# Seven-product layer 2 with gates folded into the input, in a fused attention and mixture-of-experts kernel

## Chip, cores and metric

The kernel runs on one core of one Trainium2 chip (TRN2). The metric is the device time of one execution in microseconds (us). The times quoted are medians of several executions. A profile is one execution, and its span is about 2 us shorter than that execution's time. TensorE is the matmul engine (PE in the profile; PEld is its weight load), VectorE is DVE, ScalarE is ACT, GpSimd is POOL, and SP issues most DMA transfers.

## The reference

Attention comes first: 8 batches, 8 heads, 512 local and 32 global tokens, head size 64. Local tokens see a window of 32 on each side and all global tokens. The 8 x 544 = 4352 tokens of 512 features then go through 8 experts, weighted by a gate that eight Sinkhorn iterations make.

```python
def _moe_ref(x, w_gate, w1, w2):              # x: [4352, 512], w1: [8, 512, 1024], w2: [8, 1024, 512]
    P = np.exp(x @ w_gate - max)              # [4352, 8]
    for _ in range(8):                        # Sinkhorn
        P /= P.sum(1, keepdims=True) + 1e-09
        P /= P.sum(0, keepdims=True) + 1e-09
        P *= N / E
    for e in range(E):
        h = np.maximum(x @ w1[e], 0.0)        # layer 1
        out += P[:, e:e + 1] * (h @ w2[e])    # layer 2, gated
```

All gates are positive, so P * relu(x w1) w2 is the same as relu((P * x) w1) w2. The change uses this.

## The kernel before

Three stages follow each other. (a) and (b): attention, 32 steps, one for each pair of heads; the two layers of expert 0, which need no gate yet, are cut into units that a `filler` puts between the attention instructions as soon as their tokens exist. After the last step come the Sinkhorn iterations, with more filler. (c): experts 1 to 7 over groups of 512 tokens.

```python
# (a), (b): one attention step s (pair s; the "back" of pair s-2; the "attend" of pair s-1)
if s < NP: scores(s, 0)
fill_in()
if s > READY and (s - READY - 1) % HP == 0: gate(...)       # writes the PSUM bank `gbank`, read by an exponential
if s + 1 < NP: transposes(s + 1)                            # q and k of the next pair, evicted by VectorE
if 0 <= p < NP: back(p)                                     # writes `gbank` too
if s < NP and s % 2 == 1: global_keys(b, hp // 2)           # scores of local queries against global keys
fill_in()
if s < NP: scores(s, 1); masks(s)
...
if s == HP + 2: global_prep(1)        # 12 of the 16 global blocks prepared in one piece, at pair 6
# loads: q in pieces of 256 bytes, k in pieces of 1 KB, v in pieces of 256 bytes; all global tensors at the start
```

```python
# (c): layer 1 and layer 2 of experts 1 to 7, 512 tokens at a time
def layer1(k):
    ...
    for dk in range(DP):
        nc.tensor.matmul(ph[:, ff, 0:TG], w1e[:, dk, P * fm : P * (fm + 1)], xT[:, dk, P * g0 : P * g0 + TG], ...)
    # ReLU out of PSUM: half on ScalarE, half on VectorE
def layer2(k, hT):
    for c in range(gn):               # 128 tokens: 8 matmuls of 512 columns
        for fk in range(FT):
            nc.tensor.matmul(py, hT[:, fk, P * c : P * (c + 1)], ws[e][1][:, fk, :], ...)
        nc.vector.scalar_tensor_tensor(out=out_of(to), in0=py, scalar=P_nat[:, to, e : e + 1],
                                       in1=out_of(to), op0=ALU.mult, op1=ALU.add)   # gate and add, in SBUF
```

The softmax here doesn't subtract the row's maximum and nothing guards it: scores larger than these inputs give would overflow.

Of the kernel before, what the change touches and what calls it, by code (L numbers as in the profile page):

```python
# [13 lines left out]
PSUM = bass.MemoryType.PSUM  # L14


@with_exitstack
def kernel(
# [42 lines left out]
    fill = ctx.enter_context(tc.tile_pool(name="fill", bufs=2))  # L61
    ps_mm = ctx.enter_context(tc.tile_pool(name="ps_mm", bufs=2, space=PSUM))
# [6 lines left out]
    TA = 20  # L69
    outA = persist.tile([P, TA, D], FP32)  # L70
    w1_0 = persist.tile([P, DP, F], FP16)
    w2_0 = persist.tile([P, FT, D], FP16)
    outB_box = []

    def out_of(to):
        return outA[:, to, :] if to < TA else outB_box[0][:, to - TA, :]
# [34 lines left out]
    def y_unit(g, c):  # L111
        g0, gn = groups[g]
        py = ps_mm.tile([P, D], FP32, tag="mm", name="py")
        for fk in range(FT):
            nc.tensor.matmul(py, hTs[g][:, fk, P * c : P * (c + 1)], w2_0[:, fk, :],  # L115
                             start=(fk == 0), stop=(fk == FT - 1))
        copy_to(out_of(g0 + c), py)
# [25 lines left out]
    with tc.tile_pool(name="const", bufs=1) as const, \  # L143
# [15 lines left out]
        g16 = [const.tile([P, 2 * B, Dh], FP16, name=f"g16{i}") for i in range(2)]  # L159

        stage, nat = {}, {}
        scr = outA.rearrange("p t d -> p (t d)")
        QW = H * 4 * Dh
        for n, nm in enumerate(("q", "k", "v")):
            stage[0, nm] = scr[:, QW * n : QW * (n + 1)].rearrange("p (j d) -> p j d", d=Dh)
        GW = 2 * B * Dh
        gst = [scr[:, 3 * QW + GW * n : 3 * QW + GW * (n + 1)].rearrange("p (j d) -> p j d", d=Dh) for n in range(3)]
        srcs = {"q": q_l, "k": k_l, "v": v_l}

        def load(b, nm, h0=0, h1=H):  # L170
            if (b, nm) not in stage:
                stage[b, nm] = ld.tile([P, H * NM, Dh], FP32, tag=nm + "s", name=nm + "s")
            src = srcs[nm][b, h0:h1]
            o = stage[b, nm][:, NM * h0 : NM * h1, :]
            if nm == "q":
                nc.sync.dma_start(out=o, in_=src.rearrange("h (t p) d -> p (h t) d", p=P))
            elif nm == "k":
                nc.sync.dma_start(out=o.rearrange("p (h so) d -> p h (so d)", so=4),  # L178
                                  in_=src.rearrange("h (p so) d -> p h (so d)", so=4))
            else:  # L180
                for so in range(4):
                    nc.sync.dma_start(out=o[32 * so : 32 * (so + 1)],  # L182
                                      in_=src.rearrange("h (m n so) d -> so n (h m) d", n=32, so=4)[so])
# [14 lines left out]
        def transposes(p):  # L198
            b, hp = divmod(p, HP)
            pt = ps_t.tile([P, 2, Sl], FP16, tag="t", name="pt")  # L200
            for t in range(NM):
                nc.tensor.transpose(pt[:, 0, P * t : P * (t + 1)], nat[b, "q"][:, t, 2 * hp : 2 * hp + 2, :], identity)  # L202
# [4 lines left out]
            nc.vector.tensor_copy(out=t, in_=pt)  # L207
# [120 lines left out]
        def load_g(j0, j1, eng):  # L328
            for n, src in enumerate((q_g, k_g, v_g)):
                eng.dma_start(out=gst[n][:, j0:j1, :],  # L330
                              in_=src.rearrange("b (hh hq) s d -> (hq s) (b hh) d", hq=4)[:, j0:j1, :])

        load_g(0, JA, nc.scalar)
# [8 lines left out]
        load_g(JA, 2 * B, nc.sync)  # L342
        make_identity(nc, identity)
        nc.vector.memset(gqbd, 0.0)
# [13 lines left out]
        nc.gpsimd.tensor_copy(out=vga[:, 0:JA, 0:Dh], in_=gst[2][:, 0:JA, :])  # L358
        nc.gpsimd.dma_start(out=w_gate_sb, in_=moe_w_gate.rearrange("(dko dki) e -> dki dko e", dki=P))
        tick = const.tile([P, 2], FP32)  # L360
        nc.gpsimd.tensor_copy(out=tick[:, 0:1], in_=stage[0, "v"][:, H * NM - 1, 0:1])
        nc.gpsimd.dma_start(out=w1_0, in_=moe_w1[0].rearrange("(dko dki) f -> dki dko f", dki=P))
        nc.gpsimd.tensor_copy(out=tick[:, 1:2], in_=stage[1, "k"][:, 0, 0:1])
        nc.gpsimd.dma_start(out=w2_0, in_=moe_w2[0].rearrange("(fko fki) d -> fki fko d", fki=P))

        def global_prep(part):
            j0, j1 = ((0, JA), (JA, 2 * B))[part]
            n = j1 - j0
            ceng = (nc.scalar.copy, nc.vector.tensor_copy)
            for i in (0, 1):  # L370
                ceng[i](out=g16[i][:, j0:j1, :], in_=gst[i][:, j0:j1, :])
            if part:
                nc.gpsimd.tensor_copy(out=vga[:, j0:j1, 0:Dh], in_=gst[2][:, j0:j1, :])
            JC = 4
            for j in range(j0, j1, JC):
                pq = ps_mm.tile([P, 2, 2 * JC, Sg], FP32, tag="mm", name="pq")
                for a in (0, 1):
                    for jj in range(JC):
                        flip(pq[:, a, 2 * jj : 2 * jj + 2, :], g16[a][:, j + jj, :])
                for i in (0, 1):  # L380
                    ceng[i](out=gqbd[Dh * i : Dh * (i + 1), 2 * j : 2 * (j + JC), Sg * i : Sg * (i + 1)],
                            in_=pq[Dh * i : Dh * (i + 1), 0])
                nc.scalar.copy(out=kgT[:, 2 * j : 2 * (j + JC), :], in_=pq[:, 1])
            pgg = ps_mm.tile([P, n, Sg], FP32, tag="mm", name="pgg")
# [10 lines left out]
        global_prep(0)  # L395

        LAG = 1
        READY = HP + LAG + 1
        FA = 2.6
        gA = TA // GT - 1  # L400
        for s in range(NP + LAG + 2):
            b, hp = divmod(s, HP)
            have = min((s - READY) // HP, gA)

            def fill_in():
                filler(FA / 4 if s < NP else FA / 2, have)

            if s + 1 < HP:
# [5 lines left out]
            if s > READY and (s - READY - 1) % HP == 0:  # L414
                gate((s - READY - 1) // HP)
            if s + 1 < NP:
                transposes(s + 1)
            p = s - LAG - 1
            if 0 <= p < NP:
                back(p)  # L420
            if s < NP and s % 2 == 1:
                global_keys(b, hp // 2)
# [7 lines left out]
            p = s - LAG  # L430
            if 0 <= p < NP:
                attend(p)
                if p % 2 == 1:
                    attend_g(p // HP, (p % HP) // 2)
            fill_in()
            p = s - LAG - 1
            if 0 <= p < NP and p % 2 == 1:
                back_g(p // HP, (p % HP) // 2)
# [5 lines left out]
            if s == HP + 2:  # L444
                global_prep(1)
        gate(B - 1)

    with tc.tile_pool(name="late", bufs=1, reuse_waits="tile") as late, \
         tc.tile_pool(name="wpool", bufs=2, reuse_waits="tile") as wpool, \
         tc.tile_pool(name="sink", bufs=2, reuse_waits="tile") as sink, \  # L450
         tc.tile_pool(name="ps_c", bufs=1, space=PSUM, reuse_waits="tile") as ps_c, \
         tc.tile_pool(name="ps_h", bufs=2, space=PSUM, reuse_waits="tile") as ps_h:

        outB_box.append(late.tile([P, TO - TA, D], FP32, name="outB"))
        ws = {}

        def load_w(e):
            w1e = wpool.tile([P, DP, F], FP16, tag="w1e", name="w1e")
            w2e = wpool.tile([P, FT, D], FP16, tag="w2e", name="w2e")
            nc.gpsimd.dma_start(out=w1e, in_=moe_w1[e].rearrange("(dko dki) f -> dki dko f", dki=P))  # L460
            nc.gpsimd.dma_start(out=w2e, in_=moe_w2[e].rearrange("(fko fki) d -> fki fko d", fki=P))
            ws[e] = (w1e, w2e)

        evac["eng"] = ("act",)
        load_w(1)

        cv = sink.tile([P, E], FP32, tag="c")
        nc.vector.memset(cv, 1.0)
        rv = None
        for it in range(8):  # L470
            t1 = sink.tile([P, TO, E], FP32, tag="t")
            nc.vector.tensor_tensor(out=t1, in0=K_nat, in1=cv.unsqueeze(1).broadcast_to([P, TO, E]), op=ALU.mult)
            rs = sink.tile([P, TO], FP32, tag="rs")
            nc.vector.reduce_sum(out=rs, in_=t1, axis=mybir.AxisListType.X)
            rv = sink.tile([P, TO], FP32, tag="rv")
            nc.vector.reciprocal(out=rv, in_=rs)
            t2 = sink.tile([P, TO, E], FP32, tag="t")
            nc.vector.tensor_tensor(out=t2, in0=K_nat, in1=rv.unsqueeze(2).broadcast_to([P, TO, E]), op=ALU.mult)
            cp = sink.tile([P, E], FP32, tag="cp")
            nc.vector.reduce_sum(out=cp, in_=t2.rearrange("p t e -> p e t"), axis=mybir.AxisListType.X)  # L480
            filler(3.4, len(groups))
            pcs = ps_c.tile([P, E], FP32, tag="cs")
            nc.tensor.matmul(pcs, ones_sc, cp, start=True, stop=True)
            cv = sink.tile([P, E], FP32, tag="c")
            nc.vector.reciprocal(out=cv, in_=pcs)
        t1 = sink.tile([P, TO, E], FP32, tag="t")
        nc.vector.tensor_tensor(out=t1, in0=K_nat, in1=cv.unsqueeze(1).broadcast_to([P, TO, E]), op=ALU.mult)
        nc.vector.tensor_tensor(out=P_nat, in0=t1, in1=rv.unsqueeze(2).broadcast_to([P, TO, E]), op=ALU.mult)

        evac["eng"] = ("act", "dve")  # L490
        while units:
            units.pop(0)[2]()

        outr = out.rearrange("(to p) d -> to p d", p=P)
        work = [(e, g0, gn) for e in range(1, E) for (g0, gn) in groups]

        def layer1(k):
            e, g0, gn = work[k]
            TG = gn * P
            if g0 == 0 and e + 1 < E:  # L500
                load_w(e + 1)
            w1e = ws[e][0]
            hT = fill.tile([P, FT, GT * P], FP16, tag="hT", name="hT")
# [65 lines left out]
```

## Time and profile before

| | before |
|---|---|
| time, median | 1111.41 us (4 runs), 1111.52 us (13 runs) |
| span of the profile | 1109.0 us |
| first matmul of expert 1 (start of stage c) | 281.7 us |
| last matmul starts | 1104.6 us |

The head of the page: the busy time of each engine, then TensorE's busy tenths and its granted clock (tenths of full speed) in 40 slices of the span, then the chain of work that ended last, as shares of the span.

```profile
span 1109.0 us, 15325 instructions
PE 1062.5 (96%) x6840; PEld 518.3 (47%) x6840; DVE 501.6 (45%) x719; ACT 254.8 (23%) x405; POOL 22.3 (2%) x44
...
PE   5579999899999999999999999999999999999998
...
PEclk9779999899999999999999999999999999999999
...
PE 91%; SPq 3%; DVE 2%; ACT 2%; DMA 1%; issue 1%; ACTq 0%; DVEq 0%
```

TensorE holds 91% of the chain, and only the first three slices, up to about 80 us, show holes in its row.

Groups of instructions with shapes apart (busy us, mean ns of one | idle before it). The two layers of stage (c) and what VectorE does behind them:

```profile
L527 PE MATMUL py<-w2e,hT 128*128 128x512 f16 x1904 | 421.1, 379 | 0.0
L509 PE MATMUL ph<-xT,w1e 128*128 128x512 f16 x1792 | 395.7, 379 | 0.0
L509 PE MATMUL ph<-xT,w1e 128*128 128x256 f16 x224 | 26.5, 272 | 0.0
L529 DVE SCALAR_TENSOR_TENSOR outA<-py,P_nat,outA 128x512 f32<-128x512 f32 x140 | 105.1, 751 | 112.2 <-PE py L527 111.6
```

The 379 ns are the reported length of one matmul, not its price: matmuls overlap, and their starts lie only 215.9 ns apart. The price is this distance between starts. It can be read from the chain of waits (start us, length us, what):

```profile
593.02 6.91 PE ph L509 x32
599.93 6.91 PE py L527 x32
```

A layer of 32 matmuls of 512 columns takes 6.91 us, 215.9 ns each. For the 256-column form, the records of the last group start at 1090.802, 1090.911, 1091.021 and 1091.130 us, so 109.2 ns apart where nothing waits. From the two distances, taking the price as linear in the columns, I estimate its parts: 256 columns more cost 215.9 - 109.2 = 106.7 ns, and 109.2 - 106.7 = 2.5 ns are left as a surcharge for each matmul. Stage (c) is thus bound by how many columns TensorE streams, with a small surcharge for each matmul.

The stretches 0 to 75 us (start), 75 to 222 (attention), 222 to 282 (Sinkhorn and the rest of expert 0) and 282 to 1105 us (stage c). Columns: busy us and number of instructions of PE, PEld, DVE, ACT and POOL, then the granted clock, the DMA share and GB/s:

```profile
0.00:75.00 75.00, 44.04 (x606) 26.45 (x606) 35.38 (x67) 27.75 (x59) 10.80 (x30) 0.84 1.03 218
75.00:222.00 147.00, 136.68 (x2029) 79.91 (x2028) 98.73 (x192) 82.06 (x181) 3.28 (x4) 0.95 0.48 111
222.00:282.00 60.00, 58.84 (x290) 28.75 (x289) 28.42 (x62) 21.40 (x39) 0.00 (x0) 0.98 0.08 13
282.00:1105.00 823.00, 822.95 (x3920) 383.18 (x3918) 338.32 (x398) 123.56 (x127) 8.18 (x10) 1.00 0.11 24
```

In stage (c) TensorE is busy for 822.95 of 823 us. In the first 75 us it is busy for 44, while the DMA engines are full.

### The profile page before, as it was taken

The page shows a single profiled execution, that of the slowest core. Times are in us where ns is not written, and L with a number is a line of the kernel's source. Part 1 is how long each engine was busy: PE and PEld are TensorE (multiplying, and loading weights), DVE is VectorE, ACT ScalarE, POOL GpSimd, SP SyncE. Part 2 cuts the span into 40 slices and gives each one's busy share as a digit, 9 for nine tenths or more (in the row PEclk, how much of TensorE's full clock was granted, in tenths as well). Part 3 has the DMA queues.
Part 4 walks back from the last instruction along what each step waited for, and adds up shares of the span by engine and source line. Part 5 has one row for each costly group of instructions (what it writes and reads, how often), then busy time and mean ns, then how long its engine had stood idle before and what let it go on. Part 6 is the DMA issues. An engine that isn't in the chain of part 4 may idle for free.

```text
span 1109.0 us, 15325 instructions
## 1 busy us (share of the span) xinstructions
PE 1062.5 (96%) x6840; PEld 518.3 (47%) x6840; DVE 501.6 (45%) x719; ACT 254.8 (23%) x405; POOL 22.3 (2%) x44
## 2 busy tenths in 40 slices
PE   5579999899999999999999999999999999999998
PEld 3345555544444444445444544454445444454444
DVE  5456776463355543333333343343334333333333
ACT  3355555542211111111111111111111111111110
POOL 2100000000000000000000000000000000000000
PEclk9779999899999999999999999999999999999999
DMA  9954553510000040002200220012000400001112
GB/s 220 234 137 115 153 154 77 88 28 1 1 1 1 1 76 1 1 1 39 37 1 1 38 38 1 1 33 44 1 1 1 76 1 1 1 1 76 76 76 95
DMA packets 77426, 53.42 MB, mean 48 GB/s; under 512 B 45360, under 2 KB 68912, under 8 KB 77360
## 3 DMA queue, kind: packets, MB, share of 16 engines
q1 hardware_dynamic: 62704, 35.26, 12.0%
q0 software_dynamic: 13072, 16.79, 9.5%
q8 instruction: 53, 0.87, 0.3%
q10 hardware_dynamic: 1584, 0.39, 0.2%
q14 instruction: 13, 0.11, 0.0%
HBM read 60.31 MB, written 8.91 MB: 62 GB/s over the span
## 4 chain that ended last, share of the span: by engine, by line
PE 91%; SPq 3%; DVE 2%; ACT 2%; DMA 1%; issue 1%; ACTq 0%; DVEq 0%
PE ph L509 37%; PE py L527 37%; PE ph L107 5%; PE py L115 5%; SPq L182 1%; PE sc L217 1%; SPq L330 1%; DMA qs<-in_q_l_dram 1%; PE gbank L298 1%; SPq L178 1%; PE sc L221 1%; ACT u L225 1%; PE po L256 1%; DVE u L229 1%; PE po L251 1%
## 5 line engine op out<-in xcount | busy, mean ns | idle before, releaser
L509 PE MATMUL ph<-xT,w1e 128*128 128x512 f16 (+1 forms) x2016 | 422.2, 367 | 0.0
L527 PE MATMUL py<-w2e,hT 128*128 128x512 f16 x1904 | 421.1, 379 | 0.0
L509 PEld LDWEIGHTS <-w1e 128*128 128x128 f16 x2016 | 197.2, 98 | 216.4
L527 PEld LDWEIGHTS <-hT 128*128 128x128 f16 x1904 | 186.2, 98 | 223.2
L512 ACT ACTIVATE hT<-ph 128x1024 f16<-128x1024 f32 (+1 forms) x126 | 123.1, 977 | 688.7 <-PE ph L509 688.7
L514 DVE TENSOR_SCALAR hT<-ph 128x1024 f16<-128x1024 f32 (+1 forms) x126 | 146.8, 1165 | 292.7 <-PE ph L509 292.7
L529 DVE SCALAR_TENSOR_TENSOR outA<-py,P_nat,outA 128x512 f32<-128x512 f32 x140 | 105.1, 751 | 112.2 <-PE py L527 111.6
L529 DVE SCALAR_TENSOR_TENSOR outB<-py,P_nat,outB 128x512 f32<-128x512 f32 x98 | 73.6, 751 | 80.9 <-PE py L527 80.6
L107 PE MATMUL ph<-xT,w 128*128 128x512 f16 (+1 forms) x288 | 73.6, 389 | 1.2 <-DVE outB L96 0.7
L225 ACT ACTIVATE u<-sc 128x480 f16<-128x480 f32 (+1 forms) x128 | 59.2, 516 | 41.3 <-PE sc L221 41.1
L115 PE MATMUL py<-w,hT 128*128 128x512 f16 x272 | 64.0, 379 | 0.7 <-ACT hT L88 0.7
L229 DVE TENSOR_TENSOR u<-u,mask 128x704 f16<-128x704 f16 x64 | 30.7, 522 | 34.2 <-ACT u L225 34.2
L107 PEld LDWEIGHTS <-w 128*128 128x128 f16 x288 | 26.8, 102 | 29.8 <-issue 10.1
L115 PEld LDWEIGHTS <-hT 128*128 128x128 f16 x272 | 25.5, 100 | 27.5 <-issue 1.8
L217 PE MATMUL sc<-qkT 64*128 64x160 f16 (+1 forms) x256 | 26.0, 262 | 12.3 <-DVE qkT L207 7.0
L88 ACT ACTIVATE hT<-ph 128x512 f16<-128x512 f32 (+1 forms) x45 | 26.1, 580 | 25.8 <-PE ph L107 25.4
L207 DVE COPY qkT<-pt 128x1024 f16<-128x1024 f16 x32 | 22.0, 687 | 11.9 <-PE pt L205 11.8
L299 ACT COPY xT<-gbank 128x512 f16<-128x512 f16 x32 | 18.8, 588 | 26.6 <-PE gbank L298 26.2
L90 DVE TENSOR_SCALAR hT<-ph 128x512 f16<-128x512 f32 (+1 forms) x27 | 17.5, 649 | 15.7 <-PE ph L107 15.6
L202 PE MATMUL pt<-identity,qn 128*128 128x128 f16 x128 | 13.9, 238 | 9.7 <-DVE qn L192 9.7
L272 DVE TENSOR_TENSOR xn<-po,rz 128x512 f16<-128x512 f32 x32 | 22.1, 691 | 1.1
L217 PEld LDWEIGHTS <-qkT 64*128 64x128 f16 x256 | 8.6, 96 | 28.3 <-issue 16.6
(88 smaller groups left out, 366.3 us busy)
## 6 DMA issues: line engine op xcount, KB each, us to landing
ks<-in_k_l_dram SPq DMA_DIRECT2D x7, 1024.0 KB, 5.6
vs<-in_v_l_dram SPq DMA_DIRECT2D x28, 256.0 KB, 4.7
w1e<-in_moe_w_dram POOLq DMA_DIRECT2D x7, 1024.0 KB, 7.9
w2e<-in_moe_w_dram POOLq DMA_DIRECT2D x7, 1024.0 KB, 9.0
out_dram<-outA SPq DMA_DIRECT2D x20, 256.0 KB, 2.0
out_dram<-outB SPq DMA_DIRECT2D x14, 256.0 KB, 2.0
w<-in_moe_w_dram POOLq DMA_DIRECT2D x2, 1024.0 KB, 11.3
outA<-in_q_l_dram SPq DMA_DIRECT2D x4, 256.0 KB, 5.4
```

Source lines behind the costliest of these rows:

```text
L88: nc.scalar.activation(out=o, in_=i, func=AF.Relu)
L107: nc.tensor.matmul(ph[:, 0:TG], w1_0[:, dk, P * fm : P * (fm + 1)], xT[:, dk, P * g0 : P * g0 + TG], start=(dk == 0), stop=(dk == DP - 1))
L115: nc.tensor.matmul(py, hTs[g][:, fk, P * c : P * (c + 1)], w2_0[:, fk, :], start=(fk == 0), stop=(fk == FT - 1))
L217: nc.tensor.matmul(pss[i][:, off[m] : off[m] + wid[m]], qkT[p][rr, 1, P * m : P * (m + 1)], qkT[p][rr, 0, lo[m] : hi[m]], start=True, stop ...
L225: nc.scalar.activation(out=u_[p][i][:, mp, :], in_=pss[i][:, 0:w], func=AF.Exp, scale=scale)
L229: nc.vector.tensor_tensor(out=u_[p][i][:, :, 0:HALF], in0=u_[p][i][:, :, 0:HALF], in1=mask, op=ALU.mult)
L272: nc.vector.tensor_tensor(out=t.rearrange("p t i d -> p i t d"), in0=pv[:, :, :, 0:Dh], in1=rz.unsqueeze(3).broadcast_to([P, 2, NM, Dh]), ...
L509: nc.tensor.matmul(ph[:, ff, 0:TG], w1e[:, dk, P * fm : P * (fm + 1)], xT[:, dk, P * g0 : P * g0 + TG], start=(dk == 0), stop=(dk == DP - 1))
L512: nc.scalar.activation(out=hT[:, 2 * fp : 2 * fp + 2, 0:TG], in_=ph[:, :, 0:TG], func=AF.Relu)
L514: nc.vector.tensor_scalar(out=hT[:, 2 * fp : 2 * fp + 2, 0:TG], in0=ph[:, :, 0:TG], scalar1=0.0, scalar2=None, op0=ALU.max)
L527: nc.tensor.matmul(py, hT[:, fk, P * c : P * (c + 1)], ws[e][1][:, fk, :], start=(fk == 0), stop=(fk == FT - 1))
L529: nc.vector.scalar_tensor_tensor(out=out_of(to), in0=py, scalar=P_nat[:, to, e : e + 1], in1=out_of(to), op0=ALU.mult, op1=ALU.add)
```

## The change

Its intent: fewer TensorE columns. Layer 2 of experts 1 to 7 becomes a product of 2 x 2 blocks with seven block products instead of eight (Strassen's scheme), on groups of 256 tokens. For this, the experts' results must be able to add up in PSUM without a gate, so the gate is multiplied into x. In this kernel PSUM keeps the accumulators of one group at a time and the weights of four or five experts are held at once, so there are two passes over the tokens (experts 1 to 4, then 5 to 7) with the running sum in DRAM between them. The core of it:

```diff
+    def combine_w(e):            # five sums of w2's quarters, VectorE, once per expert
+        for n, (x, y, op) in enumerate(((b11, b22, ALU.add), (b12, b22, ALU.subtract), (b21, b11, ALU.subtract),
+                                        (b11, b12, ALU.add), (b21, b22, ALU.add))):
+            nc.vector.tensor_tensor(out=wb[:, 2 + n], in0=x, in1=y, op=op)
+    PASSES = ((1, 2, 3, 4), (5, 6, 7))
+    work = [(n, g, e) for n, es in enumerate(PASSES) for g in range(GN) for e in es]      # 119 steps, 17 groups
+    def scale_x(k):              # gate, turned through DRAM to lie along the tokens, times x
+        nc.vector.tensor_tensor(out=t, in0=xT[:, :, 256 * g : 256 * (g + 1)], in1=pb..., op=ALU.mult)
     def layer1(k):
-        ... xT[:, dk, P * g0 : P * g0 + TG] ...                    # 512 columns; ReLU on ScalarE and VectorE
+        ... xps[k][:, dk, :] ...                                   # 256 columns; ReLU on ScalarE alone
+    def sum_h(k):                # five sums of h's quarters, VectorE, every step
+        for n, (x, y, op) in enumerate(((a11, a22, ALU.add), (a21, a22, ALU.add), (a11, a12, ALU.add), ...)):
+            nc.vector.tensor_tensor(out=t[:, n], in0=x, in1=y, op=op)
     def layer2(k):
-        ... 8 matmuls of 512 columns per 128 tokens, then gate and add on VectorE
+        for m in (2, 3, 0, 1, 4, 5, 6):                            # 7 products x 4 matmuls of 256 columns
+            l, r = prod[m]
+            for j in range(FK):
+                nc.tensor.matmul(acc[m // 2][:, m % 2, :], l[:, j, :], r[:, j, :], start=first, ...)
+    def finish(n, g):            # after the last expert of a pass: nine adds from PSUM, then out by DMA
...
@@ attention @@
-                nc.sync.dma_start(out=o, in_=src.rearrange("h (t p) d -> p (h t) d", p=P))      # q, 256 bytes
+                # q as k, in pieces of 1 KB; the transposes then come out permuted
-            nc.vector.tensor_copy(out=t, in_=pt)
+            nc.scalar.copy(out=t[:, 0, :].rearrange("p (n so) -> p n so", so=4), in_=pt[:, 0, :]...)   # q, reordered
+            nc.vector.tensor_copy(out=t[:, 1, :], in_=pt[:, 1, :])
-            if s == HP + 2:
-                global_prep(1)
+            if b % 2 == 1 and b + 1 < B:        # one part of four blocks at a time, in three steps
+                if hp == 1:   global_cast((b + 1) // 2) ...
+                elif hp == 2: global_flip((b + 1) // 2)
+                elif hp == 3: global_scores((b + 1) // 2)
+            # global_keys moved ahead of transposes and back; at pairs 4 and 8 the pipeline is drained first,
+            # so that the filler may start two pairs earlier; two staging buffers in rotation for q, k, v;
+            # expert 0's result leaves for DRAM
```

Six of the seven products share accumulator tiles in PSUM in pairs, and in each tile only the first matmul carries the start flag.

## The prediction

> **What bounds it now.** The chain of waits is 91% TensorE. By stage: (a) 0 to about 70 us waits for DMA. The stretches of 10 us show 180 to 270 GB/s and TensorE busy only 2 to 8 us of 10; the chain runs through SP's load issues and the landing of batch 2's q at 51 us. (b) 70 to 282 us: attention with expert 0 as filler, TensorE about 95% busy; the Sinkhorn iterations (222 to 255 us) are covered by filler. (c) 282 to 1105 us: experts 1 to 7, 3920 matmuls without one idle microsecond. The chain shows 6.91 us per 32 matmuls of 512 columns (215.9 ns each). Single starts of the 256-column form are 109.2 ns apart wherever no wait intervenes, and the weight loads (98 ns) keep up. [...] So stage (c) is bound by columns streamed.
>
> **What the change does.** Layer 2 of experts 1 to 7 becomes a seven-product (Strassen) scheme on 256-token groups: 28 matmuls of 256 columns where 32 such would be needed. Gates are folded into x, so the experts of a pass add up in PSUM; two passes, running sums through DRAM.
>
> - TensorE, stage (c): 119 steps x (32+28) = 7140 matmuls x 109.2 ns = 780 us, against 823 us. Gain 43 us. The columns alone would give 51; the doubled number of matmuls returns 8.
> - VectorE, estimated from the trace (f16 tensor-tensor of 704: 522 ns; fp32 of 272: 442; PSUM add of 512: 751): scaling x 1.2 us and five sums 2.1 us per step of 6.55 us, combining a group 5.2 us. Per group of four experts 18.4 us of 26.2, about 70%, so it should stay off the chain, with about 1 us of slack where a group's accumulators are handed over.
> - ScalarE: all ReLUs, 4 x 0.6 us per step, about 40%.
> - Weight combinations: 3.4 us of VectorE per expert, hidden, except between the passes: experts 6 and 7 are loaded only once 1 and 2 are done[...]. I expect 4 us of TensorE stall there (0 to 10).
> - DMA: running sums, gates and output add about 50 MB over 800 us, harmless.
> - Start: q moves in 1 KB packets (18 B/ns per DMA engine) instead of 256 B (12 B/ns), three quarters of the global tensors load later, and filler may begin two steps earlier. The bytes ahead of the last early wait fall from about 64 to 55 us of DMA time: gain about 9 us. The two drain steps cost perhaps 3 us back.
> - End: the last combination adds about 2 us.
>
> **Prediction.** 1111 - 43 - 9 + 3 + 4 + 2 = 1068; I lean slightly lower, as earlier filler also fills holes: **1065 us**, 8 in 10 between 1048 and 1088. Faster by over 2%: 0.90; within 2%: 0.08; slower: 0.02.
>
> **What would show it.** Steps of 60 matmuls 6.55 us apart, TensorE near 100% from the first gated layer; VectorE 65 to 75% busy there and absent from the chain; first gated layer at 270 to 275 us instead of 282; one gap of a few us two thirds of the way through, released by weight DMA or VectorE.
>
> **What would make it wrong.** VectorE or the accumulator hand-over waiting once per group (34 times 1 us already costs 34 us); a long stall between passes; weight loads not hidden behind 256-column matmuls with two different stationary sources; slow software-DMA writes of expert 0's result stalling the filler; a lower granted clock.

The rates in the text can be read from the trace of before. Packets of 256 bytes moved 12.4 B per ns and DMA engine (q from 94 to 104 us: 1.05 MB in 53% of the 16 engines' time), packets of 1 KB 18.1 (130 to 140 us: 1.27 MB in 43.8%). The software DMA queue moved 10.0 B per ns and DMA engine over the whole span (16.79 MB in 9.5%), the main hardware queue 16.6 (35.26 MB in 12.0%), at different mixes of packet sizes. The 64 and 55 us of DMA time and the gain of 9 us are estimates from such rates.

## The result and the profile after

| | before | after |
|---|---|---|
| time, median | 1111.52 us (13 runs) | 1064.24 us (8 runs, 1062.33 to 1066.77) |
| span of the profile | 1109.0 us | 1061.3 us |
| stage (c) starts | 281.7 us | 273.3 us |
| last matmul starts | 1104.6 us | 1055.4 us |
| stage (c), from the two lines above | 822.9 us | 782.1 us |
| from there to the end | 4.4 us | 5.9 us |

The ratio of after to before is 0.9576 (95% interval 0.9566 to 0.9586). The outputs are right. Ratios here are the mean time of one kernel's fast runs over that of the other's in the same rounds, so not quite the ratio of the medians. Between the profiles the span falls by 47.7 us: 40.8 in stage (c), 8.4 ahead of it, and 1.5 given back at the end.

The head of the page of after:

```profile
span 1061.3 us, 23417 instructions
PE 1017.0 (96%) x10063; PEld 831.7 (78%) x10063; DVE 654.4 (62%) x1381; ACT 450.1 (42%) x825; POOL 48.0 (5%) x88
```

The weight loads rose from 47% to 78% of the span because in stage (c) there are 7140 of them instead of 3918, each of 98 ns as before. The groups of stage (c), shapes not kept apart:

```profile
L580 PE MATMUL ph<-xp,w1e 128*128 128x256 f16 x3808 | 435.0, 273 | 2.4 <-ACT h L582 1.3
L604 PE MATMUL acc<-wb,s 128*128 128x256 f16 x2380 | 279.2, 273 | 0.0
L604 PE MATMUL acc<-wb,h 128*128 128x256 f16 x952 | 123.4, 273 | 0.0
L590 DVE TENSOR_TENSOR s<-h 128x512 f16<-128x512 f16 x595 | 210.0, 420 | 255.8 <-ACT h L582 255.8
L568 DVE TENSOR_TENSOR xp<-xT,pb 128x1024 f16<-128x1024 f16 x119 | 145.0, 1219 | 31.7 <-DMA pb<-ptd 31.7
L629 DVE TENSOR_TENSOR o<-o,acc 128x256 f32<-128x256 f32 (+1 forms) x306 | 134.4, 504 | 6.5 <-PE ph L580 1.8
```

3808 + 2380 + 952 = 7140 matmuls, and 2.4 us of idle in front of them all. VectorE waits for ScalarE's ReLU for 255.8 us, so it has time to spare. One step in the chain of after:

```profile
592.86 3.49 PE ph L580 x32
596.35 3.06 PE acc L604 x28
```

A step is 3.49 + 3.06 = 6.55 us without a gap, as it is at nearly all 119 steps. The weight loads of 98 ns stay hidden: the matmuls of stage (c) start 109.2 ns apart. The stretches that answer to those of before (start, attention, Sinkhorn and rest of expert 0, stage c):

```profile
0.00:75.00 75.00, 52.98 (x683) 31.77 (x684) 38.61 (x79) 36.28 (x78) 10.66 (x32) 0.82 1.00 248
75.00:217.00 142.00, 133.12 (x1988) 77.11 (x1987) 91.69 (x188) 90.51 (x203) 10.88 (x21) 0.99 0.37 107
217.00:273.00 56.00, 50.72 (x260) 24.25 (x257) 32.98 (x68) 18.10 (x35) 13.63 (x19) 1.00 1.00 194
273.00:1055.60 782.60, 780.17 (x7143) 698.55 (x7140) 489.10 (x1043) 305.25 (x511) 12.85 (x18) 1.00 0.28 77
```

In stage (c) VectorE is busy 489.1 / 782.6 = 62%, ScalarE 39%, the clock is at 1.00. In the first 75 us TensorE is busy 53.0 us instead of 44.0. So the 8.4 us ahead of stage (c) come from the first part; the DMA engines are still full there (share 1.00). Two obvious rivals, more filler done early and a better clock, do not show in the two traces: the first scores of pair 8 start at 77.5 us before and at 67.4 us after, and up to that point both have run the same 32 matmuls of filler and have had the granted clock at half for the same time (23.9 and 24.0 us).

Of the gaps in stage (c), one stands at the change of pass. The chain there, in order of time:

```profile
727.21 3.01 DVE wb L504 x5
730.22 1.15 DVE xp L568
731.37 0.14 issue
731.50 3.65 PE ph L580 x32
```

The combinations of expert 7's weights (wb) stand ahead of the scaling of x (xp) in VectorE's program order, and TensorE waits for that: its starts at 730.14 and 731.50 us are 1.36 us apart, 1.25 more than the regular distance. The other gap (283.24 to 284.85 us, 1.5 more than the regular distance) lies at the very beginning, where ScalarE sits idle for 4.9 us until the stored result of expert 0 has landed and does the next ReLUs only after scaling it.

### The profile page after: what moved, and what is told of

Its sections match the earlier page's. It is cut to its first block, busy times and chain, and to the rows that moved or that the text cites. A ratio compares the mean times of both kernels' runs of the same rounds, so it can differ in the third digit from the quotient of the medians.

```text
span 1061.3 us, 23417 instructions
## 1 busy us (share of the span) xinstructions
PE 1017.0 (96%) x10063; PEld 831.7 (78%) x10063; DVE 654.4 (62%) x1381; ACT 450.1 (42%) x825; POOL 48.0 (5%) x88
## 4 chain that ended last, share of the span: by engine, by line
PE 71%; DVE 1%; issue 0%; ACT 0%; DVEq 0%
PE ph L580 38%; PE acc L604 33%; DVE o L629 1%; DVE wb L504 0%; DVE s L590 0%; DVE xp L568 0%; ACT h L582 0%; DVEq L721 0%; DVEq L629 0%; DVEq L504 0%
## 5 line engine op out<-in xcount | busy, mean ns | idle before, releaser
L582 ACT ACTIVATE h<-ph 128x512 f16<-128x512 f32 x476 | 283.8, 597 | 466.2 <-PE ph L580 427.8
L580 PE MATMUL ph<-xp,w1e 128*128 128x256 f16 x3808 | 435.0, 273 | 2.4 <-ACT h L582 1.3
L580 PEld LDWEIGHTS <-w1e 128*128 128x128 f16 x3808 | 372.5, 98 | 46.1 <-issue 2.9
L590 DVE TENSOR_TENSOR s<-h 128x512 f16<-128x512 f16 x595 | 210.0, 420 | 255.8 <-ACT h L582 255.8
L604 PE MATMUL acc<-wb,s 128*128 128x256 f16 x2380 | 279.2, 273 | 0.0
L604 PEld LDWEIGHTS <-s 128*128 128x128 f16 x2380 | 232.9, 98 | 27.0
L568 DVE TENSOR_TENSOR xp<-xT,pb 128x1024 f16<-128x1024 f16 x119 | 145.0, 1219 | 31.7 <-DMA pb<-ptd 31.7
L629 DVE TENSOR_TENSOR o<-o,acc 128x256 f32<-128x256 f32 (+1 forms) x306 | 134.4, 504 | 6.5 <-PE ph L580 1.8
L604 PE MATMUL acc<-wb,h 128*128 128x256 f16 x952 | 123.4, 273 | 0.0
L115 PEld LDWEIGHTS <-hT 128*128 128x128 f16 x272 | 25.5, 98 | 27.1 <-issue 0.4
```

The source lines that it names most:

```text
L115: nc.tensor.matmul(py, hTs[g][:, fk, P * c : P * (c + 1)], w2_0[:, fk, :], start=(fk == 0), stop=(fk == FT - 1))
L568: nc.vector.tensor_tensor(out=t, in0=xT[:, :, 256 * g : 256 * (g + 1)], in1=pb.unsqueeze(1).broadcast_to([P, DP, 256]), op=ALU.mult)
L580: nc.tensor.matmul(ph[:, ff, :], w1e[:, dk, P * fm : P * (fm + 1)], xps[k][:, dk, :], start=(dk == 0), stop=(dk == DP - 1))
L582: nc.scalar.activation(out=hT[:, 2 * fp : 2 * fp + 2, :], in_=ph, func=AF.Relu)
L590: nc.vector.tensor_tensor(out=t[:, n], in0=x, in1=y, op=op)
L604: nc.tensor.matmul(acc[m // 2][:, m % 2, :], l[:, j, :], r[:, j, :], start=first, stop=(e == es[-1] and j == FK - 1), skip_group_check=True)
```

## The experiments

Twelve kernels ran, all correct, each timed in rounds together with the kernel before. All are edits of the changed kernel, so a ratio is to be compared with 0.9576, and a difference of 0.001 is 1.1 us. The intervals of single ratios are about 0.002 to each side, so less than 2.5 us is not resolved by the times alone. There is a second yardstick for the start: five profiles with an unchanged start (after, prod8_256, prod8_512, scale2, scale3) begin stage (c) at 273.3, 275.3, 275.4, 276.8 and 274.1 us, on average 275.0. The start's gain is then 281.7 - 275.0, about 7 us, though only one profile of before stands against five, and four of the five come from a session in which the kernel before itself took 1114.3 us, not 1111.5. From the times alone, (1 - 0.9576) x 1111.5 = 47.1 us in all, less 40.8 in stage (c), plus 1.5 at the end, it is about 8 us. Because sessions differ in this way, an absolute time in an expectation is best compared through its ratio.

### Is stage (c) bound by columns? Eight products in the new structure

```diff
-        for m in (2, 3, 0, 1, 4, 5, 6): ... 28 matmuls of 256 columns, sums of h and of w2 on VectorE
+        for a in (0, 1):
+            for c in range(0, D, W):                  # W = 256, or 512 in the second kernel
+                for fk in range(FT):
+                    nc.tensor.matmul(acc[a][:, c : c + W], hT[:, fk, P * a : P * (a + 1)], w2[:, fk, c : c + W], ...)
```

> The changed kernel with layer 2 in eight plain products of 256 columns (32 matmuls per step instead of 28), without the sums on VectorE and without the weight combinations; gating, two passes and PSUM accumulation stay. Theory (stage c is bound by the columns that TensorE streams): step 64 x 109.2 ns = 6.99 us instead of 6.55 us, 119 steps, so 52 us more, less up to 3 us for the gaps that the combinations caused: 1114 us. Rival (the gain comes from the new structure: no gating and no read-add-write per expert on VectorE, accumulation in PSUM): about 1064 us, or less, as VectorE is relieved further.

Measured: 1114.87 us beside 1114.28 us of before, ratio 1.0013 (0.9992 to 1.0035). That is (1.0013 - 0.9576) x 1111.5 = 49 us more than the changed kernel.

> As the eight-product kernel, but layer 2 in 16 matmuls of 512 columns. Theory: layer 2 takes 16 x 215.9 = 3.45 us against 32 x 109.2 = 3.49 us, so 119 x 0.04 = 5 us less than with 256 columns: 1109 us. That is the price of the doubled matmul count for one layer, by itself. Rival (a fixed cost per matmul does not matter): the same time as with 256 columns. The new structure without the seven products then stands within 3 us of the kernel before.

Measured: 1109.16 us, ratio 0.9956 (0.9936 to 0.9976), 42 us more. The chains of the two, first with 256 and then with 512 columns:

```profile
595.30 3.49 PE ph L572 x32
598.80 3.49 PE acc L586 x32
```

```profile
593.62 3.49 PE ph L572 x32
597.12 3.45 PE acc L586 x16
```

All of the gain in stage (c) hangs on the seventh product that is not there. The new structure by itself, with gating, passes and PSUM accumulation, stands no more than half a per cent below the kernel before, although VectorE is busy for only 31% of the span in the 256-column kernel. The surcharge for twice as many matmuls in one layer is 3.49 - 3.45 us a step in the chains; the times of the two kernels differ by 6 us, as expected within their intervals.

### How much slack has VectorE?

```diff
-        nc.vector.tensor_tensor(out=t, in0=xT[...], in1=pb..., op=ALU.mult)
+        for _ in range(2):                            # 3 in the second kernel
+            nc.vector.tensor_tensor(out=t, in0=xT[...], in1=pb..., op=ALU.mult)
```

> The changed kernel with the scaling of x done twice (1.22 us more VectorE work per step of 6.55 us; result unchanged). Theory (VectorE off the chain, 61% busy per group of four experts, sums ready about 2 us before TensorE asks for them): 1064 to 1067 us. Rival (VectorE or the accumulator hand-over is nearly on the chain): over 1080 us.

In the trace of the changed kernel the sums are ready 1.1 us ahead of the first matmul that reads them at the tightest step, early in stage (c) (288.07 to 289.21 us), and 4.8 us ahead in a steady one (566.04 to 570.86 us).

Measured: 1072.70 us, ratio 0.9622 (0.9598 to 0.9645), 5 us more than the changed kernel: just above the expected range and far below the rival's.

> Scaling done three times. VectorE then has 25.8 us of work in 26.2 us of a group in the first pass, and 20.4 us in 19.65 us in the second. Theory: the second pass becomes VectorE-bound, 17 x 0.7 = 12 us, and the weight combinations (13 us in the first pass against 7 us of slack) add 5 to 8 us: about 1083 us. Rival (VectorE still hidden): 1066 us; rival (VectorE nearly on the chain already): 119 x 2.4 us more, over 1200 us.

Measured: 1102.27 us, ratio 0.9904 (0.9880 to 0.9928), 36 us more; more than expected. What TensorE waits for in stage (c) (total us, times, longest us), first scaled twice, then three times:

```profile
PE ph L581 <- DVE xp L569: 3.8, 2, 3.6
PE ph L581 <- ACT h L583: 2.9, 1, 2.9
```

```profile
PE ph L581 <- DVE xp L569: 26.7, 34, 5.4
PE ph L581 <- ACT h L583: 4.5, 1, 4.5
```

Scaled twice, VectorE has 20.9 us of work in the 26.2 us of a group in the first pass, 80%, and by the same count 16.7 in 19.65 us in the second, 85%. The steady steps then show no gap (one early step lost 0.4 us). The two one-off places got longer: the first, ScalarE's wait for expert 0's stored result, by 1.5 us, the second, where the weight combinations compete, by 2.5. Scaled three times, the load is 98% in the first pass and 104% in the second; nearly every group of both passes then has one gap with starts 0.78 us apart, 0.67 us more than regular, and the one-off places take the rest. My estimate had let the first pass through because its work still fitted into a group on average; it did not ask whether each piece is ready in time. So VectorE is off the chain in the changed kernel, the steady steps give way somewhere between 85% and 98% of load, and no wait for the accumulator hand-over is listed in stage (c).

In these two profiles a long gap cost more than its own length. During the four longest gaps (starts 3.1 to 5.7 us apart) the granted clock fell to half and stayed there for 3.4 to 6.8 us; the matmuls after the gap then started 0.21 us apart instead of 0.109. Gaps of up to 2.8 us had no such effect there; in the trace of before, starts 4.1 us apart (at 27.6 us) had none either. In the profile of the kernel scaled twice, the slowest of its four runs, the halved clock is 4 of the 8.5 us by which stage (c) is longer than in the changed kernel.

### What made the start shorter? The reasons of the prediction

```diff
# q256
+            if nm == "q":
+                nc.sync.dma_start(out=o, in_=src.rearrange("h (t p) d -> p (h t) d", p=P))
...
-            nc.scalar.copy(out=t[:, 0, :].rearrange("p (n so) -> p n so", so=4), in_=...)
+            nc.scalar.copy(out=t[:, 0, :], in_=pt[:, 0, :])
```

> The changed kernel with q loaded in 256-byte pieces again, as before the change (the transposes then come out in natural order). Theory (the first 75 us wait for DMA; a 256-byte packet moves 12 B per ns on each DMA engine, a 1 KB packet 18): 1.9 us more DMA time per batch, three batches ahead of the last early wait: 4 to 6 us more, 1068 to 1070 us. Rival (the start gains from the earlier filler): unchanged, 1064 us.

Measured: ratio 0.9585 (0.9567 to 0.9603), 1 us more, stage (c) at 274.6 us: no effect that these runs can see.

```diff
# gall
+        for part in (1, 2, 3):
+            load_g(part, nc.sync)         # right behind batch 1, into a part of xT that is not yet written
```

> The changed kernel with all the global tensors loaded at the start, as before the change (three of four parts, 1.2 MB in 256-byte packets, about 6 us of DMA time; they land in a part of x that is not yet used). Theory (start bound by DMA): about 4 us more (two of the three parts, as the second part is early in both), 1067 to 1070 us. Rival: unchanged.

Measured: ratio 0.9567 (0.9551 to 0.9584), stage (c) at 276.7 us: no effect.

```diff
# nodrain
-        DRAIN = (HP, 2 * HP)
+        DRAIN = ()
-            have = b - 1 if s < 3 * HP else (s - READY) // HP
+            have = (s - READY) // HP
```

> The changed kernel without the two drain steps, filler starting two pairs later as before the change. Theory of the prediction (filler that starts earlier fills holes, the drains cost 3 us): between 2 us less and 3 us more. Rival (the earlier filler is the main gain of the start): 5 us more or above, 1069 us or above.

Measured: ratio 0.9562 (0.9541 to 0.9584), 1.6 us less, which is not resolved. Stage (c) starts at 271.2 us in this profile, earlier than in any of the five of the yardstick, but at 276.2 us in the profile of the last kernel below, which has no drains either. The earlier filler brings nothing that these runs can see; whether the drains cost anything stays open.

So none of the three reasons that I gave for the start holds up when it is undone alone. They were not undone together, so a sum of shares too small to be resolved is not excluded.

### What else could it be?

A fourth candidate came from the trace of before, where TensorE waits for batch 2's q up to 53 us. Its load was issued only at 43.3 us; I put that down to the wait for a staging buffer, which the trace does not show (SP lists no such wait there, and was issuing the loads of the global tensors until 43.1 us). The two longest waits of TensorE from 40 to 75 us in that trace are this one and one inside the preparation of the global blocks:

```profile
PE sc L217 <- DVE qkT L207: 7.0, 2, 6.6
PE pq L305 <- DVE g L371: 2.9, 1, 2.9
```

In the changed kernel neither is listed in that stretch, and the longest wait is 1.9 us. The staging undone:

```diff
# stage1
-                stage[b, nm] = ld.tile([P, H * NM, Dh], FP32, tag=nm + "s", bufs=2, name=nm + "s")
+                stage[b, nm] = ld.tile([P, H * NM, Dh], FP32, tag=nm + ("s" if b else "s0"), name=nm + "s")
```

> The changed kernel with the staging of q, k, v as before the change: batch 0 in buffers of its own and one buffer for each of the others, instead of two in rotation. Theory (before, batch 2's q could be loaded only once batch 1's had been cast; TensorE waited 6.9 us for it, 46.2 to 53.1 us in the trace before): 4 to 7 us more, ratio 0.961 to 0.964, first gated layer at about 280 us. Rival (preparation block): unchanged, 0.957.

Measured: ratio 0.9569 (0.9546 to 0.9591), stage (c) at 271.8 us: this theory fell too.

```diff
# prep_block (on top of gall)
-            if b % 2 == 1 and b + 1 < B: ... one part at a time, in three steps
+            if s == HP + 2:
+                for part in (1, 2, 3):
+                    global_cast(part); global_flip(part); global_scores(part)
```

> The changed kernel with all global tensors loaded at the start (measured alone: no effect) and the preparation of the last three parts in one block at pair 6, as before the change. Theory (the block holds TensorE, 62.3 to 69.4 us in the trace before, with 5.9 us of idle time; spread over three batches it is hidden): 4 to 7 us more, ratio 0.961 to 0.964, first gated layer at about 280 us instead of 275. Rival (staging, below): unchanged, 0.957.

Measured: ratio 0.9627 (0.9610 to 0.9644), 5.7 us more than the changed kernel and 6.7 us more than gall, from which it differs in this alone; stage (c) at 279.8 us. TensorE's longest waits from 55 to 75 us in it:

```profile
PE pgg L399 <- ACT kgT L391: 4.0, 3, 1.3
PE gbank L295 <- DVE xn L269: 2.2, 2, 1.4
PE pq L302 <- DVE g L378: 2.1, 1, 2.1
PE pq L302 <- ACT g L378: 1.4, 2, 0.7
```

The block is a chain of small casts, flips, copies and products, with TensorE waiting at each hand-over: 4.0 + 2.1 + 1.4 = 7.5 us. Cut into three steps that lie a whole attention step apart, most of these waits are gone: gall lists only 1.1 us at such hand-overs there, though 6.3 us at other places. That the block costs time in the new order is shown by the times. How much of the 6.7 us is the waits is not: up to pair 8 the granted clock was at half for 37.0 us here and for 22.7 us in gall, and stage (c) starts only 3.1 us later than in gall's profile. Nor is the block quite that of the kernel before, whose trace lists 5.0 us of such waits (62.3 to 69.4 us; the expectation above had 5.9).

### The global-key scores: a wait moved, and what it was worth

```diff
# keys_back
-            if s < NP and s % 2 == 1:
-                global_keys(b, hp // 2)
             if s + 1 < NP:
                 transposes(s + 1)
             if not (s in DRAIN or s - 1 in DRAIN):
                 finish_pair(s - 2, "b")
+            if s < NP and s % 2 == 1:
+                global_keys(b, hp // 2)
```

> The changed kernel with the global-key scores put back to their old place, after the transposes and the back step. The trace after shows a wait that was not there before: TensorE waits 10.1 us in total for the exponentials before these matmuls. Theory (that wait is on the chain, as TensorE is 95% busy in attention): up to 8 us less, 1056 to 1062 us. Rival (the wait only moves, since the same score buffers are needed by the next matmuls): unchanged within 2 us.

Measured: ratio 0.9658 (0.9641 to 0.9675), 9 us more instead of 8 us less: both theories missed, and the move is a gain in itself. TensorE's longest waits from 55 to 216 us, first in the changed kernel, then with the keys back:

```profile
PE pgk L232 <- ACT u L222: 8.7, 9, 1.9
PE gbank L295 <- DVE xn L269: 1.7, 2, 0.9
```

```profile
PE gbank L295 <- ACT K_nat L320: 6.2, 5, 1.9
PE sc L214 <- ACT ugk L235: 5.4, 8, 0.9
PE gbank L295 <- DVE og L288: 2.2, 4, 0.9
```

At their new place the key scores take the wait for the exponentials (8.7 us), which looked like something to remove. But they also stand between `gate`, whose result an exponential reads out of `gbank`, and `back`, which writes `gbank` again. At the old place `back` waits for that exponential (6.2 us), and the next scores wait for the keys' own (5.4 us). The listed waits differ by only a few us; the time differs by 9. In the profile of keys_back the granted clock from 105 to 135 us is 0.81 to 0.89, against 1.00 in the changed kernel, and there pairs 14 and 15 take 19.4 us instead of 15.1. This is one profile; the mean clock of the five timed runs went from 0.977 to 0.986 while their times lay within 1.9 us, so that this share of the loss comes from the clock is not shown. Note also that in the kernel before, where the keys stood at the old place, `back` waited only 0.6 us for that exponential: the move removes a wait that is large only together with other parts of the new order.

```diff
# keys_dve (on top of keys_back)
-            nc.scalar.copy(out=t[:, 0, :].rearrange("p (n so) -> p n so", so=4), in_=...)
+            nc.vector.tensor_copy(out=t[:, 0, :].rearrange("p (n so) -> p n so", so=4), in_=...)
```

> Global-key scores at their old place, as in keys_back (ratio to the kernel before 0.966, against 0.958 for the changed kernel), and q's share of the transposes evicted by VectorE as before instead of ScalarE. Theory (the old place is costly only because the new ScalarE copy stands ahead of the exponential of the global keys, 0.6 us in each of 16 places, about 9 us): ratio back to about 0.958. Rival (the order on TensorE is what matters): ratio stays near 0.966.

Measured: ratio 0.9633 (0.9615 to 0.9652). Some 3 of the 9 us may come from the new ScalarE copy in front of the exponentials (the intervals overlap, and what the copy costs on VectorE instead is not measured); the larger part stays with the order on TensorE.

### A version meant to beat both

```diff
# best (on top of nodrain)
     load_o(0, 0)
-    scale_o(0, 0)
     sum_h(0)
...
-        if k + 2 < len(work):
-            scale_x(k + 2)
+        if k == 1:
+            scale_o(0, 0)
+        for j in (k + 2, k + 3) if n == 0 and g == GN - 1 and e in (3, 4) else (k + 2,):
+            if j < len(work) and j not in xps:
+                scale_x(j)
```

> A version meant to beat both: no drain steps (alone: ratio 0.956, first gated layer 2 to 5 us earlier), the scaling of expert 0's stored result moved off ScalarE's way at the first gap (1.4 us), and x scaled one step ahead at the change of pass (1.3 us). Theory: both gaps of TensorE in the gated stage vanish, 3 to 6 us less than the changed kernel: ratio 0.953 to 0.955. Rival: the gaps reappear elsewhere, 0.956.

Measured: 1061.82 us beside 1111.87 us of before, ratio 0.9551 (0.9531 to 0.9570), about 2.8 us better than the changed kernel, at the edge of what the intervals separate, and not separated from the kernel without drains (0.9562). The profile is clearer for stage (c). These are TensorE's waits from 270 us on, first in the changed kernel, then in this one:

```profile
PE ph L580 <- ACT h L582: 1.3, 1, 1.3
PE ph L580 <- DVE xp L568: 1.1, 1, 1.1
```

```profile
PE ph L107 <- DVE ys L96: 0.4, 1, 0.4
```

Both gaps are gone (the wait that is left belongs to expert 0), and stage (c) takes 1055.6 - 276.2 = 779.4 us instead of 782.1, which is 7140 x 109.2 ns = 779.7 us to within the rounding. The start shows no gain: in this profile stage (c) begins 2.9 us later than in the changed kernel's.

## Why the prediction was right, and where its reasons were not

The time was predicted at 1065 us and measured at 1064.24. The terms add up to 1068; the last 3 us were a lean on the earlier filler, for which no run shows a gain, so a hit this close is luck. Term by term:

- **TensorE in stage (c), -43 us, and stalls, +4.** Right in kind and size. Measured were -40.8 in all; without the two gaps, which cost 2.8, it would have been 43.5. The step was predicted and measured at 6.55 us, and the eight-product kernels show that nothing but the missing product brings the gain. Of the 4 us of stall, all expected at the change of pass, 1.25 came there; 1.5 came at the first step, by ScalarE's wait for a DMA, which I had not foreseen.
- **VectorE off the chain.** Right. The sizes were a little high: 59% busy in the first pass (400 to 700 us) where 70% was estimated, nine adds in 4.05 us where 5.2 were, five sums in 1.77 us where 2.1 were. I had used the reported durations of single instructions; instructions in a row start closer together than that: in the trace after 336 ns apart for the sums (420 reported) and 602 ns for the weight combinations (685 reported).
- **Start, -9 +3 = -6 us.** The net size fits (about -7 to -8), the reason does not. The step that failed is "The bytes ahead of the last early wait fall from about 64 to 55 us of DMA time: gain about 9 us". The DMA engines were busy (share 1.03 in the first 75 us), and so I took them for the bound. Undone alone, neither q's piece size (1 us, though packets of 1 KB moved 18.1 B per ns and DMA engine and those of 256 bytes 12.4) nor the time of the global loads (-1 us) changed anything that the runs resolve. In their place the runs show two pieces of TensorE ordering, each undone in the new kernel: the preparation of the global blocks spread out (5.7 us) and the key scores moved ahead (9 us). Together these are more than the start gained, so other parts of the new schedule must cost something or the effects overlap. The ScalarE copy (perhaps 3 us) is a candidate that the runs point to. How the rest adds up is open, as is what each part would bring in the kernel before: all were undone in the changed kernel, one at a time, and effects of this kind need not add.
- **End, +2 us.** Measured 1.5.

The total was right partly because the one wrong reason had the right net size. An argument that is checked by the total alone would not have shown it.

## What to carry to other kernels

Where TensorE streams without a gap, price a change in columns plus a fixed amount per matmul, both read from distances between starts (here 106.7 ns for 256 columns and 2.5 ns per matmul), and check first that every other engine has time to spare under that pace; a load of 80 to 85% left the steady steps untouched here, 98% did not. A full DMA row in a start-up phase did not by itself make DMA the bound here (share 1.0, and the two supposed causes, undone, moved the time by +1 and -1 us): undo the supposed cause and see. And a wait that the profile newly lists need not be a loss: the instruction that waits may stand there in place of two that would have waited elsewhere.
